# Attention's 64-row matmuls gathered in runs, and layer products handed out chunk by chunk

## Chip, core and metric

The kernel runs on one core of a Trainium2 chip. The metric is the device time of one execution in microseconds (us), the median of several runs. A second number is used below: the profiler's record of one execution, whose span begins with the first and ends with the last recorded instruction.

The engines are TensorE (PE in the profile), its weight loads (PEld), VectorE (DVE), ScalarE (ACT), GpSimd (POOL, idle here) and SyncE (SP), whose queue issues all DMAs. Each engine works through its own instructions in the order in which they stand in the program.

## What is computed

Sigmoid attention, then two feed-forward blocks, all in float32:

```
scores = q @ k.T / sqrt(64) - log(448)         # 4 batches x 12 heads, 448 tokens, head size 64
x = sigmoid(scores) @ v                        # heads laid side by side: 1792 x 768
h = maximum(maximum(x @ w1, x @ w2), x @ w3)   # 768 x 768 each
y = h @ w_out                                  # 768 x 768
t = y @ w_in                                   # 768 x 2048
out = (t * sigmoid(1.702 * t)) @ w_out2        # 2048 x 768
```

## The kernel before

**Precision.** A float32 operand is split into a rounded part (hi) and the rest (lo), and a product is three matmuls: hi by hi, hi by lo, lo by hi. The copies that make hi run on ACT or DVE, whichever the planner gives them to (`copy`); the subtractions that make lo run on DVE alone (`rest`). The six head pairs in `PLAIN` use the sigmoids unsplit.

**Attention.** Two heads make a pair `p`; there are 24 pairs, six to a batch. A pair has four steps `c` over its keys. In steps 0 to 2, `score` issues six matmuls with 64 contraction rows (L412): the two heads lie in rows 0 to 63 and 64 to 127 of the array, and the matmuls of the two heads run side by side, two in the time of one. Step 3 has the last 64 keys of both heads in one 128-row matmul, three times (L414). The scores of a step land in one of two PSUM buffers `sc`, ACT makes the sigmoid `a` from it (L419), and copies and rests make `ah` and `al`. `weigh` multiplies by v into PSUM `av`: 128-row matmuls in steps 0 to 2 (L446, or L438 for plain pairs), 64-row matmuls in step 3 of a pair that isn't plain (L450). `finish` turns `av` into the hi and lo of `x`, one chunk of the contraction (of six) for the first layers.

**Layers.** For each batch `b`, `unit1` runs 18 products for w1, w2, w3 and their maximum, `unit2` six for w_out. Each takes one weight tile `w1` from a ring of five buffers. In batch 0 the tiles are decoded by ACT and DVE (`new_weights`: one ACT and four DVE instructions, then a copy and a rest) and also written to DRAM (`kept`); in batches 1 to 3 they are loaded from there. `product` (L357) issues the 18 matmuls of a tile (six chunks `k`, three each, L363 to L365) as one operation, so it begins only when all six chunks of x are there. Then `unit3` and `unit4` do the last two layers (L553 to L555) over all batches.

**What sets the order.** Nothing is ordered by hand on the engines. The code records operations with what they read and write. `Order.run` then plays a plan: each TensorE operation has a due time (the sum of the planned times of those recorded before it), other operations inherit one from what needs them, and each engine takes the ready operation that is due first. DVE takes a copy that ACT could do as well only as if it were due 12 us later (`SLACK`). The order so found is the program's order, fixed. The order of recording: `step(p, c)` scores step c of pair p and weighs step c of pair p - 1; 28 steps are recorded ahead of the first layer, and the others are spread over the layer units of batches 0 to 2 (L593).

Of the kernel before, what the change touches and what calls it, by code (L numbers as in the profile page):

```python
# [8 lines left out]
F32R = mybir.dt.float32r  # L9
# [6 lines left out]
P = 128  # L16
B, H, S, D = 4, 12, 448, 64
DM = H * D
DFF = 2048
KC = DM // P  # L20
NF = DFF // P
NPAIR = H // 2
NP = B * NPAIR
# [10 lines left out]
MM = 0.201  # L34
# [58 lines left out]
class Order:  # L93
# [35 lines left out]
    def run(self):  # L129
        for r in self.rings:  # L130
            for old, new in zip(r.tiles, r.tiles[r.n :]):
                first = min(new.ops, key=lambda o: o.n)
# [9 lines left out]
        while stack:  # L142
            o = stack.pop()
            seen += 1
            took = min(o.on.values())
# [7 lines left out]
        free = {"PE": 0.0, "ACT": 0.0, "DVE": 0.0, "SP": 0.0, "-": 0.0}  # L153
        need = {o: len(o.pre) for o in self.ops}
# [3 lines left out]
        def offer(o):  # L158
            for e in o.on:
                heapq.heappush(ready[e], (o.late + (SLACK if e == "DVE" and len(o.on) > 1 else 0.0), o.n, o))  # L160
# [5 lines left out]
        while len(done) < len(self.ops):  # L166
            for e in free:
                while free[e] <= now + 1e-9 and ready[e]:
                    _, _, o = heapq.heappop(ready[e])
                    if o in done:  # L170
                        continue
                    done.add(o)
                    o.fn(e)
                    if e == "SP":
                        bus = max(bus, now) + o.on[e]
                        end, free[e] = bus + 2.0, now + 0.07
                    else:
                        end = free[e] = now + o.on[e]
                    o.began, o.end = now, end
                    serial += 1  # L180
                    heapq.heappush(events, (end + o.lag, serial, o))
                    heapq.heappush(events, (free[e], -serial, None))
            assert events, f"{len(self.ops) - len(done)} operations that never begin"
            now = max(now, events[0][0])
            while events and events[0][0] <= now + 1e-9:
                _, _, o = heapq.heappop(events)
                for x in o.post if o is not None else ():
                    need[x] -= 1
                    if not need[x]:
                        offer(x)  # L190


def moe_chain_kernel(tc, qk, vv, v4, wa, wb, out):
# [3 lines left out]
    O = Order()  # L197
# [4 lines left out]
    def ring(p, name, shape, n, dtype=F32, gate=None):  # L202
        return O.ring(n, lambda: p[0].tile(shape, dtype, name=name, tag=name, bufs=n), gate)
# [62 lines left out]
    ]  # L266
    ts, his, los, a2s, a1s, ah2s, ah1s, al2s, al1s, vfs, vss, v4s, xfs, folds = att_rings
    xs = [ring(xp, f"x{k}", [P, 2, S], 2, F32R) for k in range(KC)]
    w1s = ring(xp, "w1", [P, 2, DM], 5, F32R)
    hs = [ring(mid, f"h{k}", [P, 2, S], 1, F32R) for k in range(KC)]  # L270
    mxs = ring(mid, "mx", [P, S], 2)
    yst = ring(mid, "yst", [P, 2, S], 2, F32R)

    def banks(p, name, n, shape=(P, 512)):
        return O.ring(n, lambda: p[0].tile(list(shape), F32, name=name, tag=name, bufs=n))
# [79 lines left out]
        return hi, lo  # L355

    def product(ps, w, x):  # L357
        def f(_):
            wh, wl = w[0](), w[1]()
            for k in range(KC):  # L360
                c = slice(k * P, (k + 1) * P)
                xh, xl = x[k][0](), x[k][1]()
                pe.matmul(ps(), wh[:, c], xh, start=k == 0, stop=False)  # L363
                pe.matmul(ps(), wh[:, c], xl, start=False, stop=False)  # L364
                pe.matmul(ps(), wl[:, c], xh, start=False, stop=k == KC - 1)  # L365

        return O.pe(f, 3 * KC * MM, [*w, *(y for z in x for y in z)], [ps])


    X = [[] for _ in range(B)]  # L370
# [1 line left out]
    class Pair:  # L372
# [27 lines left out]
        def score(self, c):  # L400
# [4 lines left out]
            def f(_):  # L405
                o, h, l = ps(), self.h(), self.l()
                for n, (kx, qx) in enumerate(((h, h), (h, l), (l, h))):
# [5 lines left out]
                    if not pair:  # L413
                        pe.matmul(o, kx[:, keys], qx[:, :S], **how)  # L414

            a, n = (a2s if pair else a1s).tile().part(), (2 if pair else 1) * S
            used = (0, 1 + c // 2) if self.p == 0 else (0,)
            O.pe(f, 3 * MM, [x[i] for x in (self.hi, self.lo) for i in used], [ps])
            on("ACT", t_act(n) + 0.07, lambda: act.activation(a(), ps(), AF.Sigmoid, bias=bias, scale=scale), [ps], [a])  # L419
            self.a[c] = [a]  # L420
            if not self.plain:
# [5 lines left out]
        def weigh(self, c):  # L427
# [22 lines left out]
                            pe.matmul(av[e](), w, x()[r, :], start=False, stop=n == 1)  # L450

            took = (2 if c < 3 else 1) * 0.75 if self.plain else (4 if c < 3 else 2) * MM
            O.pe(plain if self.plain else parts, took, [*self.v, *a], av)
            if c == 3:
                self.finish()

        def finish(self):
            b, hp = divmod(self.p, NPAIR)
# [22 lines left out]

    pairs = [None] * NP

    def step(p, c):
        if p < NP:
            if c == 0:
                pairs[p] = Pair(p)
            pairs[p].score(c)
        if p > 0:
            pairs[p - 1].weigh(c)  # L490


    HS, mx = [None] * KC, [None]
# [88 lines left out]
            pe.matmul(mm_warm(), warm()[:, 0, :P], warm()[:, 1], start=n == 0, stop=n == WARM - 1)  # L582

    O.pe(warming, 3.7, [warm], [mm_warm])
    steps = [(p, c) for p in range(NP + 1) for c in range(4)]
    at = 4 * (NPAIR + 1)
    for s in steps[:at]:
        step(*s)
    order = [(1, m, e) for m in range(KC) for e in range(3)] + [(2, m, 0) for m in range(KC)]
    for b in range(B):  # L590
        first = at
        for n, (layer, m, e) in enumerate(order):
            while b < B - 1 and at < min(len(steps), first + -(-24 * (n + 1) // 22), 28 + 24 * (b + 1)):  # L593
                step(*steps[at])
                at += 1
            unit1(b, m, e) if layer == 1 else unit2(b, m)
    first_ops = {o for r in (*att_rings, scs, avs) for t in r.tiles for o in t.ops}
# [85 lines left out]
```

## Time and profile before

| | us |
|---|---|
| median of 3 runs (1016.23 to 1017.87) | 1017.61 |
| the profiled execution, whole | 1015.61 |
| its recorded span | 1013.8 |
| PE busy in the span | 998.4 |
| DVE busy | 619.5 |
| ACT busy | 360.5 |

The profiled execution was 2.0 us shorter than the median of the three timed runs. The span falls into stretches: attention alone until 65 us, attention with batch 0's layer products and weight decoding until about 198 us, attention with batches 1 and 2 until 442 us, the rest of batches 2 and 3 until 538 us, then the last two layers. A PE that counts as busy is not always at its peak: matmuls overlap, so the distance between the starts of neighbours, not the duration of one, tells the pace.

### The profile page before, as it was taken

The page shows a single profiled execution, that of the slowest core. Times are in us where ns is not written, and L with a number is a line of the kernel's source. Part 1 is how long each engine was busy: PE and PEld are TensorE (multiplying, and loading weights), DVE is VectorE, ACT ScalarE, POOL GpSimd, SP SyncE. Part 2 cuts the span into 40 slices and gives each one's busy share as a digit, 9 for nine tenths or more (in the row PEclk, how much of TensorE's full clock was granted, in tenths as well). Part 3 has the DMA queues.
Part 4 walks back from the last instruction along what each step waited for, and adds up shares of the span by engine and source line. Part 5 has one row for each costly group of instructions (what it writes and reads, how often), then busy time and mean ns, then how long its engine had stood idle before and what let it go on. Part 6 is the DMA issues. An engine that isn't in the chain of part 4 may idle for free.

```text
span 1013.8 us, 12189 instructions
## 1 busy us (share of the span) xinstructions
PE 998.4 (98%) x4918; PEld 864.8 (85%) x4918; DVE 619.5 (61%) x936; ACT 360.5 (36%) x523; POOL 1.1 (0%) x6
## 2 busy tenths in 40 slices
PE   8899999999999999999999999999999999999998
PEld 5457877888888888899998999999999999999997
DVE  6988889865654455455511356776747676664444
ACT  7775767443543444332212342222212122121110
POOL 0000000000000000000000000000000000000000
PEclk9999999999999999999999999999999999999999
DMA  7788677985548554499867211110201111000023
GB/s 253 229 288 285 232 283 288 388 336 170 203 161 289 188 165 140 158 314 414 308 222 274 108 63 63 61 65 1 94 32 63 63 63 63 1 1 1 1 93 125
DMA packets 39656, 165.95 MB, mean 164 GB/s; under 512 B 4400, under 2 KB 10288, under 8 KB 39600
## 3 DMA queue, kind: packets, MB, share of 16 engines
q1 hardware_dynamic: 39600, 165.17, 45.8%
q8 instruction: 39, 0.64, 0.3%
q14 instruction: 17, 0.14, 0.0%
HBM read 129.76 MB, written 35.39 MB: 163 GB/s over the span
## 4 chain that ended last, share of the span: by engine, by line
PE 97%; ACT 1%; DMA 1%; DVE 0%; issue 0%; SPq 0%; DVEq 0%; ACTq 0%
PE mm L363 19%; PE mm L365 19%; PE mm L364 19%; PE po L554 8%; PE po L555 8%; PE po L553 8%; PE av L446 5%; PE sc L412 5%; PE av L438 3%; PE sc L414 1%; PE av L450 1%; ACT a L419 1%; DMA v<-in_v 1%; DMA t<-in_qk 0%; ACT fold L470 0%
## 5 line engine op out<-in xcount | busy, mean ns | idle before, releaser
L363 PE MATMUL mm<-x,w 128*128 128x448 f32 x432 | 161.0, 373 | 0.0
L364 PE MATMUL mm<-x,w 128*128 128x448 f32 x432 | 157.8, 365 | 0.0
L365 PE MATMUL mm<-x,w 128*128 128x448 f32 x432 | 157.6, 365 | 0.0
L553 PE MATMUL po<-g,w 128*128 128x448 f32 x384 | 140.4, 366 | 1.3 <-ACT g L217 1.3
L365 PE MATMUL mm<-z,w 128*128 128x448 f32 x384 | 141.4, 368 | 0.0
L363 PE MATMUL mm<-z,w 128*128 128x448 f32 x384 | 141.3, 368 | 0.0
L364 PE MATMUL mm<-z,w 128*128 128x448 f32 x384 | 141.2, 368 | 0.0
L554 PE MATMUL po<-g,w 128*128 128x448 f32 x384 | 140.4, 366 | 0.2 <-DVE g L220 0.2
L555 PE MATMUL po<-g,w 128*128 128x448 f32 x384 | 140.1, 365 | 0.0
L220 DVE TENSOR_TENSOR acc<-po,acc 128x448 f32<-128x448 f32 (+1 forms) x169 | 104.5, 621 | 53.5 <-PE po L555 52.8
L537 ACT ACTIVATE sg<-mm 128x448 f32<-128x448 f32 x64 | 34.8, 544 | 258.6 <-PE mm L365 258.6
L419 ACT ACTIVATE a<-sc,bias 128x896 f32<-128x896 f32 (+1 forms) x96 | 87.3, 915 | 93.3 <-PE sc L412 68.0
L220 DVE TENSOR_TENSOR al<-a,ah 128x896 fp32r<-128x896 f32 (+1 forms) x72 | 69.7, 974 | 49.2 <-ACT ah L217 48.8
L220 DVE TENSOR_TENSOR gf<-mm,sg 128x448 f32<-128x448 f32 x64 | 39.9, 624 | 97.0 <-ACT sg L537 96.5
L363 PEld LDWEIGHTS mm<-x,w 128*128 128x128 f32 x432 | 81.1, 188 | 10.7 <-issue 3.3
L364 PEld LDWEIGHTS mm<-x,w 128*128 128x128 f32 x432 | 81.2, 188 | 7.3 <-issue 1.1
L365 PEld LDWEIGHTS mm<-x,w 128*128 128x128 f32 x432 | 81.1, 188 | 6.4
L553 PEld LDWEIGHTS po<-g,w 128*128 128x128 f32 x384 | 72.1, 188 | 7.5 <-ACT g L217 1.6
L365 PEld LDWEIGHTS mm<-z,w 128*128 128x128 f32 x384 | 72.2, 188 | 6.8
L364 PEld LDWEIGHTS mm<-z,w 128*128 128x128 f32 x384 | 72.2, 188 | 6.7
L363 PEld LDWEIGHTS mm<-z,w 128*128 128x128 f32 x384 | 72.2, 188 | 6.6
L554 PEld LDWEIGHTS po<-g,w 128*128 128x128 f32 x384 | 72.1, 188 | 6.2 <-DVE g L220 0.5
(76 smaller groups left out, 1363.6 us busy)
## 6 DMA issues: line engine op xcount, KB each, us to landing
w<-kept SPq DMA_DIRECT2D x72, 768.0 KB, 4.8
raw<-in_wb SPq DMA_DIRECT2D x32, 768.0 KB, 5.2
raw<-in_wa SPq DMA_DIRECT2D x24, 768.0 KB, 6.0
kept<-w SPq DMA_DIRECT2D x24, 768.0 KB, 5.3
t<-in_qk SPq DMA_DIRECT2D x23, 480.0 KB, 3.7
yk<-yst SPq DMA_DIRECT2D x24, 448.0 KB, 5.0
z<-yk SPq DMA_DIRECT2D x24, 448.0 KB, 8.5
out_t<-acc SPq DMA_DIRECT2D x23, 224.0 KB, 1.9
```

The source lines that it names most:

```text
L220: return on("DVE", t_two(n), lambda: dve.tensor_tensor(to(), a(), b(), op=op), [a, b], [to])
L363: pe.matmul(ps(), wh[:, c], xh, start=k == 0, stop=False)
L364: pe.matmul(ps(), wh[:, c], xl, start=False, stop=False)
L365: pe.matmul(ps(), wl[:, c], xh, start=False, stop=k == KC - 1)
L412: pe.matmul(o[:, e, :], kx[r, keys], qx[r, :S], **how)
L419: on("ACT", t_act(n) + 0.07, lambda: act.activation(a(), ps(), AF.Sigmoid, bias=bias, scale=scale), [ps], [a])
L438: pe.matmul(o, w, x[:, e, :] if c < 3 else x, start=c + e == 0, stop=c == 3)
L446: pe.matmul(av[e](), w, x()[:, e, :], start=c + n == 0, stop=False)
L537: on("ACT", t_act(S), lambda sg=sg, ps=ps: act.activation(sg(), ps(), AF.Sigmoid, scale=1.702), [ps], [sg])
L553: pe.matmul(ps(), wh[:, c], gh, start=j == 0, stop=False)
L554: pe.matmul(ps(), wh[:, c], gl, start=False, stop=False)
L555: pe.matmul(ps(), wl[:, c], gh, start=False, stop=j == 1)
```

## The change

`beat(n)` takes the place of `step`. Three beats serve two pairs. Each beat begins with a `group`: the 64-row matmuls of two score steps, and with them, where a pair that isn't plain ends, its 64-row weighing of step 3, recorded as one TensorE operation that needs all its inputs and both `sc` buffers. Behind it a beat records the 128-row work: the scores of step 3 (`last_keys`) and the weighing of steps 0 to 2 (`weigh`). Eleven beats stand ahead of the first layer, the other 27 are spread over batches 0 to 2, more densely in batch 1.

`product` records six operations of three matmuls, one for each chunk, so a product may begin when the first chunk of x is there, and others may stand between its chunks. In the planner, a TensorE operation that follows another on TensorE alone no longer waits the planned 0.25 us. The ring of `w1` shrinks from five to four buffers, the ring `yst` grows from two to three.

```diff
-                    heapq.heappush(events, (end + o.lag, serial, o))
-                    heapq.heappush(events, (free[e], -serial, None))
+                    heapq.heappush(events, (end + o.lag, serial, o, False))
+                    heapq.heappush(events, (free[e], -serial, o if e == "PE" else None, True))
...
                 for x in o.post if o is not None else ():
-                    need[x] -= 1
-                    if not need[x]:
-                        offer(x)
+                    if same == ("PE" in o.on and "PE" in x.on):
+                        need[x] -= 1
+                        if not need[x]:
+                            offer(x)
...
-    w1s = ring(xp, "w1", [P, 2, DM], 5, F32R)
+    w1s = ring(xp, "w1", [P, 2, DM], 4, F32R)
...
-    yst = ring(mid, "yst", [P, 2, S], 2, F32R)
+    yst = ring(mid, "yst", [P, 2, S], 3, F32R)
...
     def product(ps, w, x):
-        def f(_):
-            wh, wl = w[0](), w[1]()
-            for k in range(KC):
-                c = slice(k * P, (k + 1) * P)
-                xh, xl = x[k][0](), x[k][1]()
+        for k, (hi, lo) in enumerate(x):
+            c = slice(k * P, (k + 1) * P)
+
+            def f(_, k=k, c=c, hi=hi, lo=lo):
+                wh, wl, xh = w[0](), w[1](), hi()
                 pe.matmul(ps(), wh[:, c], xh, start=k == 0, stop=False)
-                pe.matmul(ps(), wh[:, c], xl, start=False, stop=False)
+                pe.matmul(ps(), wh[:, c], lo(), start=False, stop=False)
                 pe.matmul(ps(), wl[:, c], xh, start=False, stop=k == KC - 1)
 
-        return O.pe(f, 3 * KC * MM, [*w, *(y for z in x for y in z)], [ps])
+            O.pe(f, 3 * MM, [*w, hi, lo], [ps])
...
+    def group(scores, ends=()):
+
+        made = [(p, c, heads(p).score(c)) for p, c in scores if p < NP]
+        whole = [p for p in ends if heads(p).plain]
+        all_ = [m for _, _, m in made] + [heads(p).weigh(3) for p in ends if p not in whole]
+
+        def f(e):
+            for m in all_:
+                m[0](e)
+
+        O.pe(f, sum(m[1] for m in all_) + SWITCH, [x for m in all_ for x in m[2]], [x for m in all_ for x in m[3]])
+        for p, c, m in made:
+            heads(p).scored(c, m[3][0])
+        for p in whole:
+            O.pe(*heads(p).weigh(3))
+        for p in ends:
+            heads(p).finish()
...
+    def beat(n):
+
+        p, part = n // 3 * 2, n % 3
+        if part == 0:
+            group([(p, 0), (p, 1)], [p - 2] if p > 1 else [])
+            weigh(p - 1, 0, 1, 2)
+        elif part == 1:
+            group([(p, 2), (p + 1, 0)], [p - 1] if p > 0 else [])
+            last_keys(p)
+            weigh(p, 0, 1)
+        else:
+            group([(p + 1, 1), (p + 1, 2)])
+            last_keys(p + 1)
+            weigh(p, 2)
...
-    steps = [(p, c) for p in range(NP + 1) for c in range(4)]
-    at = 4 * (NPAIR + 1)
-    for s in steps[:at]:
-        step(*s)
+    beats = NP // 2 * 3 + 2
+    at = 9 + 2
+    for n in range(at):
+        beat(n)
...
-            while b < B - 1 and at < min(len(steps), first + -(-24 * (n + 1) // 22), 28 + 24 * (b + 1)):
-                step(*steps[at])
+            while b < B - 1 and at < min(beats, first + -(-9 * (n + 1) // (17 if b else 22))):
+                beat(at)
                 at += 1
```

What this makes of TensorE's order in batch 1, where layer products (`mm`) and attention alternate. Before (L412 is a 64-row score step of six matmuls, L446 a 128-row weighing):

```order
L412 MATMUL sc_2413<-qh_2189 128x448 x2
L412 MATMUL sc_2413<-ql_2214,qh_2189 128x448 x2
L412 MATMUL sc_2413<-qh_2189,ql_2214 128x448 x2
L446 MATMUL av_2423<-ah2_2273,vs_2212 128x448
L446 MATMUL av_2425<-ah2_2273,vs_2212 128x448
L446 MATMUL av_2423<-al2_2276,vs_2212 128x448
L446 MATMUL av_2425<-al2_2276,vs_2212 128x448
L412 MATMUL sc_2432<-qh_2189 128x448 x2
L412 MATMUL sc_2432<-ql_2214,qh_2189 128x448 x2
L412 MATMUL sc_2432<-qh_2189,ql_2214 128x448 x2
```

After, in the same stage (L413 are the score steps, L454 the 64-row weighing of step 3, L364 the next layer matmul):

```order
L413 MATMUL sc_2566<-qh_2427 128x448 x2
L413 MATMUL sc_2566<-ql_2444,qh_2427 128x448 x2
L413 MATMUL sc_2566<-qh_2427,ql_2444 128x448 x2
L413 MATMUL sc_2573<-qh_2427 128x448 x2
L413 MATMUL sc_2573<-ql_2444,qh_2427 128x448 x2
L413 MATMUL sc_2573<-qh_2427,ql_2444 128x448 x2
L454 MATMUL av_2421<-ah1_2437,vs_2274 128x448
L454 MATMUL av_2423<-ah1_2437,vs_2274 128x448
L454 MATMUL av_2421<-al1_2453,vs_2274 128x448
L454 MATMUL av_2423<-al1_2453,vs_2274 128x448
L364 MATMUL mm_2540<-x4_1545,w1_2389 128x448
```

Two score steps and the weighing of a third pair now stand in one row. In the whole program TensorE's order has 78 unbroken rows of 64-row matmuls before and 38 now; the number of matmuls is the same.

TensorE's order among the first pairs, where attention stood alone. Before (L450 is a 64-row weighing, and no layer matmul stands ahead of the 146th row of the order):

```order
L414 MATMUL sc_289<-qh_201 128x448
L414 MATMUL sc_289<-ql_215,qh_201 128x448
L414 MATMUL sc_289<-qh_201,ql_215 128x448
L450 MATMUL av_252<-ah1_250,vs_147 128x448
L450 MATMUL av_254<-ah1_250,vs_147 128x448
L450 MATMUL av_252<-al1_270,vs_147 128x448
L450 MATMUL av_254<-al1_270,vs_147 128x448
L412 MATMUL sc_306<-qh_258 128x448 x2
```

After (L364 to L366 are a layer product's first chunk, x0, with the first weight tile):

```order
L454 MATMUL av_237<-ah1_263,vs_138 128x448
L454 MATMUL av_239<-ah1_263,vs_138 128x448
L454 MATMUL av_237<-al1_283,vs_138 128x448
L454 MATMUL av_239<-al1_283,vs_138 128x448
L364 MATMUL mm_311<-x0_222,w1_182 128x448
L365 MATMUL mm_311<-x0_222,w1_182 128x448
L366 MATMUL mm_311<-x0_222,w1_182 128x448
L415 MATMUL sc_321<-qh_188 128x448
```

The first chunk of the first product stands among the first pairs' steps, at row 58 of the order.

DVE's order ahead of the last (24th) weight tile that batch 0 decodes. Before (L336 is the last decoding instruction, the last row the tile's rest):

```order
L220 TENSOR_TENSOR al2_1752<-a2_1621,ah2_1689 128x448
L220 TENSOR_TENSOR yst_1748<-mm_1710,yst_1748 128x448
L336 SCALAR_TENSOR_TENSOR y_1706<-raw_1652,y_1706 128x768
L474 TENSOR_TENSOR xf_1789<-av_1613,fold_1780 64x448
L474 TENSOR_TENSOR xf_1789<-av_1615,fold_1783 64x448
L220 TENSOR_TENSOR w1_1793<-y_1706,w1_1793 128x768
```

After:

```order
L221 TENSOR_TENSOR yst_1838<-mm_1794,yst_1838 128x448
L337 SCALAR_TENSOR_TENSOR y_1829<-raw_1748,y_1829 128x768
L221 TENSOR_TENSOR al2_1881<-a2_1708,ah2_1791 128x896
L221 TENSOR_TENSOR vs_1853<-vf_1622,vs_1853 128x7x64
L221 TENSOR_TENSOR al2_1911<-a2_1798,ah2_1860 128x896
L221 TENSOR_TENSOR w1_1906<-y_1829,w1_1906 128x768
```

The tile's rest is DVE's row 231 of the order before and its row 250 now: more of attention's work stands ahead of it.

## Rows read from the trace of the kernel before

**Rows 1.** The profile page's head and part 1: engine, busy us (share), instructions.
```profile
span 1013.8 us, 12189 instructions
PE 998.4 (98%) x4918; PEld 864.8 (85%) x4918; DVE 619.5 (61%) x936; ACT 360.5 (36%) x523; POOL 1.1 (0%) x6
```

**Rows 2.** Stretches: length, busy by engine, granted clock, DMA share, GB/s.
```profile
0.00:65.00 65.00, 58.05 (x265) 33.33 (x266) 52.60 (x75) 48.64 (x64) 1.08 (x6) 1.00 0.74 252
65.00:198.00 133.00, 130.68 (x641) 106.60 (x640) 120.00 (x169) 85.58 (x116) 0.00 (x0) 1.00 0.80 290
```

**Rows 3.** PE's waits over the span: us in total, times, longest.
```profile
PE sc L412 <- ACT a L419: 5.6, 6, 1.4
PE av L438 <- DMA v<-in_v: 1.8, 1, 1.8
...
PE po L553 <- ACT g L217: 1.3, 1, 1.3
PE sc L414 <- ACT a L419: 0.5, 1, 0.5
```

**Rows 4.** Timeline of PE, one 64-row run: start, us, line, tiles, shapes, count.
```profile
252.51 0.37 PE L414 MATMUL sc<-qh,ql 128*128 128x448 f32 x1
252.81 0.47 PE L450 MATMUL av<-ah,vs 64*128 64x448 f32 x2
253.12 0.36 PE L450 MATMUL av<-al,vs 64*128 64x448 f32 x2
253.41 0.47 PE L363 MATMUL mm<-x,w 128*128 128x448 f32 x1
253.72 0.36 PE L364 MATMUL mm<-x,w 128*128 128x448 f32 x1
```

**Rows 5.** Timeline of PE inside a run of two score steps.
```profile
35.79 0.37 PE L412 MATMUL sc<-qh,ql 64*128 64x448 f32 x2
35.99 0.37 PE L412 MATMUL sc<-qh 64*128 64x448 f32 x2
36.20 0.37 PE L412 MATMUL sc<-ql,qh 64*128 64x448 f32 x2
```

**Rows 6.** Timeline of PE: begin of the first and of the last 64-row run.
```profile
5.18 0.47 PE L412 MATMUL sc<-qh 64*128 64x448 f32 x2
...
441.95 0.47 PE L450 MATMUL av<-ah,vs 64*128 64x448 f32 x2
```

**Rows 7.** The page's costliest groups: the sigmoids on ACT; busy, mean ns | idle before.
```profile
L419 ACT ACTIVATE a<-sc,bias 128x896 f32<-128x896 f32 (+1 forms) x96 | 87.3, 915 | 93.3 <-PE sc L412 68.0
```

**Rows 8.** Groups of instructions by line: attention's rests and copies on DVE.
```profile
L220 DVE TENSOR_TENSOR al<-a,ah 128x896 fp32r<-128x896 f32 (+1 forms) x72 | 69.7, 974 | 49.2 <-ACT ah L217 48.8
...
L220 DVE TENSOR_TENSOR vs<-vf,vs 128x448 fp32r<-128x448 f32 x18 | 11.1, 619 | 0.0
...
L217 DVE CAST qh<-t 128x960 fp32r<-128x960 f32 (+1 forms) x17 | 10.5, 615 | 18.7 <-PE sc L414 13.2 <-DMA t<-in_qk 5.5
...
L217 DVE CAST ah<-a 128x896 fp32r<-128x896 f32 (+1 forms) x10 | 5.1, 508 | 0.6 <-ACT a L419 0.5
```

**Rows 9.** DVE's waits from 0 to 198 us, the longest three.
```profile
DVE y L331 <- ACT y L323: 7.4, 8, 1.8
DVE qh L217 <- DMA t<-in_qk: 5.5, 2, 3.7
DVE mx L220 <- PE mm L365: 3.6, 6, 0.9
```

**Rows 10.** Timeline of DVE: the rest of the 24th weight tile.
```profile
187.87 0.96 DVE L220 TENSOR_TENSOR w<-y,w 128x768 fp32r<-128x768 f32 x1 [0.18 <-ACT w L217]
```

**Rows 11.** Timeline of PE: the first matmul with the 24th weight tile.
```profile
192.91 0.36 PE L363 MATMUL mm<-h,w 128*128 128x448 f32 x1
```

**Rows 12.** Timeline of PE: a plain pair's first weighing, behind its load of v.
```profile
71.11 1.77 PE L438 MATMUL av<-a,v 128*128 128x448 f32 x4 [1.84 <-DMA v<-in_v]
```

**Rows 13.** The page's DMA issues: KB each, median us from issue to landing.
```profile
w<-kept SPq DMA_DIRECT2D x72, 768.0 KB, 4.8
```

## What the change should do to the time

> **What bounds the kernel now.** I read the page's busy times first: PE is busy for 998.4 of 1013.8 us, DVE for 619.5 and ACT for 360.5 [rows 1]. So time can only be won where PE works at less than its pace or waits. The list of waits is next: the waits of PE that the profile names for the sigmoids, for a load of v and at the begin of the last layers add up to 5.6 + 0.5 + 1.8 + 1.3 = 9.2 us [rows 3]. That is 1% of the span; the rest must be sought inside the busy time.
>
> The timeline of PE shows it. Among full matmuls the starts are 0.20 us apart, and so are those of 64-row pairs inside a run: 35.79, 35.99, 36.20 [rows 5]. At the two edges of a 64-row run the distances are longer [rows 4]: from the last full matmul (252.51) to the first 64-row pair 0.30, from that to the next pair 0.31, from the last pair (253.12) to the full matmul 0.29, from that to its neighbour 0.31. Each is some 0.10 us more than 0.20, four times: **one run of 64-row matmuls costs 0.41 us on top of its work**, and this run had no wait in it. PE counts as busy meanwhile, so no list of waits shows it. Such runs go from 5.18 to 441.95 us, 78 of them [rows 6]: 78 x 0.41 = 32 us of the busy time are edges.
>
> The third view is DVE by stretches, since it is the engine that the change may load: 52.6 of the first 65 us and 120.0 of the next 133 [rows 2], 90% in the stretch in which it decodes batch 0's weights. Behind that it has room: 619.5 - 52.6 - 120.0 = 447 us in the other 816.
>
> **The change part by part.**
>
> *Grouping.* TensorE's order has 38 runs now, 40 fewer. The steps inside a longer run keep the 0.20 us pace [rows 5], whether they use the same tiles or not, and the number of matmuls stays. All of it is on the path, since PE is: **40 x 0.41 = 16.4 us less**. From below: if a run of three different steps had an edge of its own inside, of half the price, 36 groups would pay some 0.2 us each and 7 us would be left out of 16.4. Rows 5 speak against it, the two steps there write different score buffers and the pace doesn't change; I take 16.4.
>
> *Score buffers.* A group needs both `sc` buffers, so it waits for the sigmoids of the two steps before it, and everything behind it on PE waits too. Two steps take PE 1.2 us (six pairs of 0.20), the two sigmoids take ACT 2 x 0.915 [rows 7]. What covers the difference is the 128-row work between two groups. From the order, at 0.20 us a matmul and some 1.5 us a plain step: 1.5 to 4.4 us ahead of the second to the ninth group, 3.7 us or more (mostly 8 to 10) after that. So only the first groups can wait for ACT, as the single steps did before: the waits for sigmoids came to 6.1 us in 7 waits [rows 3]. The earlier first chunks of the layers now lie among these steps and fill some of that. Bounds: all 6.1 us gone, or as much again. I take no difference, because the work between the first groups is no shorter than that which stood between the single steps there (1.4 to 3 us, worked out alike).
>
> The Trainium skill has a rule against this part. Its page TensorEngine Tiling (Array Packing), section PSUM Bottleneck, says that tiling speeds up TensorE but not the emptying of PSUM, and that the copy out of PSUM can become the bound. The trace shows the same order of sizes here, 1.83 us for ACT against 1.2 for PE; what the rule would make of the time is the first rival below.
>
> *Chunks.* A product was one operation and is six; they carry the same 18 matmuls at the same pace, and no other engine sees the seams. Price nothing; what they bring is the filling just named. They also open two products early, whose weight tiles then stay occupied until the last chunk of x comes.
>
> *Weights in batch 0.* Before, the 24th tile was ready at 187.87 + 0.96 = 188.83 us [rows 10] and first used at 192.91 [rows 11]: 4.1 us to spare. I priced both orders up to these two points by rows. PE has 535 full matmuls, 129 pairs and 36 edges ahead of it before, 550, 146 and 22 now; the plain matmuls are equal. That is 32 x 0.20 - 14 x 0.41 = 0.8 us more: what the edges save there, more attention uses up. DVE has 19 more instructions ahead of it: 11 copies and 8 rests. At 0.51 to 0.62 us a copy and 0.62 to 0.97 a rest [rows 8] that is about 6.2 and 6.4 us. With all of it the tile would be 12.6 - 0.8 - 4.1 = 7.7 us late, and PE, which has it next, would stand. But a copy is given to DVE only where nothing more urgent is ready, so the copies should fall into its waits (7.4 us for ACT's part of the decoding, 5.5 for the first loads, 3.6 for layer products [rows 9]). With the rests alone it is 6.4 - 0.8 - 4.1 = 1.5 us late. Bounds 0 (the rests too go into waits) and 8 us; I take **3 us more**, near the lower end for that reason.
>
> *Four weight buffers instead of five.* From batch 1 on a tile is loaded in 4.8 us [rows 13]. Three others are used meanwhile, 18 matmuls of 0.20 each, 11 us. Covered twice over; if that cover were gone each late tile would cost the difference, some us in all. Nothing.
>
> *v4 has one buffer still.* A plain pair's v is loaded only when the plain pair before has been weighed; that cost 1.8 us once [rows 12]. By the order the work between the two is 4.7 us instead of 4.3. Nothing to 0.4 us won. The third `yst` buffer frees a wait of ACT's that PE doesn't share: nothing. The begin of the last layers has a wait of 1.3 us [rows 3] for the activations; other chunks stand there now that wait for loads instead. I leave it as it is.
>
> **The sum.** 1015.6 - 16.4 + 3 = 1002.2 us for an execution like the profiled one. The runs' median is 2.0 us above that one, so **1004 us** for the median. 0.2% (2 us) is about what a measurement of this kernel can tell from no change.
>
> **The rivals.**
>
> *Slower: the score buffers bind (6%).* If the groups had nothing to cover their sigmoids, each would wait 1.83 - 1.2 = 0.6 us: 36 x 0.6 = 22 us, more than the 16.4 saved, and the median would be 1017.6 - 16.4 + 22 = 1023. It turns the sign once the mean wait of a group is above 16.4 / 36 = 0.46 us. For it: groups ask for both buffers at once, and ACT also makes copies between the sigmoids. It is what the rule on PSUM of the Trainium skill, TensorEngine Tiling (Array Packing), comes to here. Against it: gaps of 8 to 10 us between most groups, and ACT busy for 86 of 133 us [rows 2].
>
> *DVE takes most of it back (8%).* Batch 0's decoding sets the pace: each of the 24 tiles comes late in turn, and 8 to 14 us are lost instead of 3: 1009 to 1016. For it: 90% busy, and 4.1 us to spare where 12.6 us more stand ahead. Against it: by then DVE has waited for 7.4 + 5.5 + 3.6 us and more [rows 9], and nothing forces those waits to stay.
>
> *No change (5%).* The edges are not saved, because the extra 0.10 us is paid by each change of tile inside a group as well, or because waits make up for it by chance: 1016 to 1019.
>
> *Better (5%).* The first chunks fill most of the early waits and DVE is never late: 1004 - 3 - 6 = 995, or under.
>
> **How the numbers follow.** The forecast's own case, 996 to 1009, has 76%. It spans 3 us of DVE less or 5 more than taken and the early waits filled in part. The range of 996 to 1012 adds the nearer half of the DVE case: about 80%. Faster by over 0.2%: 76 + 8 + 5 = 89%. Within 0.2%: 5%. Slower: 6%.
>
> **What would show it.** In the profile of the changed kernel, PE's busy time should be near 982 us, the starts at the edges of a run should still be 0.30 apart and those inside 0.20, over about 38 runs. PE's waits for sigmoids should lie in the first 50 us and not exceed some 6 us. The step on DVE is right if PE's waits for weight tiles or for `al` between 65 and 200 us come to 0 to 8 us, and wrong if there are none or many more. The forecast is wrong if the 64-row pairs inside a run are 0.30 us apart, if groups in batch 1 wait for ACT, or if loads of weights are waited for after 350 us.

## The result, and the profile after

The changed kernel takes **1002.85 us** (median of four runs, 1001.56 to 1004.32) against 1017.37 us for the kernel before in the same comparison (1016.23 to 1017.87): a ratio of 0.9859, 95% interval 0.9842 to 0.9876. The forecast of 1004 us was 1.2 us too high. One of the four executions of `e6_late` below, at 3879.44 us, stands alone and is not counted. The profiled execution of after took 1004.32 us, the longest of its four, with a span of 1002.5 us; span against span the profiles differ by 11.3 us. So the two differences, of medians (14.5) and of profiles (11.3), are not the same, and both have to be explained.

The page's head and its first part for the kernel after (engine, busy us, share, instructions), which answer [rows 1]:

```profile
span 1002.5 us, 12196 instructions
PE 987.9 (99%) x4918; PEld 872.3 (87%) x4918; DVE 621.9 (62%) x945; ACT 347.1 (35%) x514; POOL 1.1 (0%) x6
```

PE has as many matmuls as before and is busy for 10.5 us less: the gain lies inside the busy time. The prediction had expected 982.

The stretches of after that answer [rows 2] (length, busy by engine, clock, DMA share, GB/s):

```profile
0.00:65.00 65.00, 56.82 (x264) 36.75 (x266) 55.06 (x81) 40.84 (x52) 1.08 (x6) 1.00 0.75 261
65.00:198.00 133.00, 131.37 (x676) 109.99 (x673) 123.09 (x174) 91.36 (x127) 0.00 (x0) 1.00 0.74 269
```

In the first 65 us PE is busy for 1.2 us less than before and DVE for 2.5 us more. In the next stretch PE stands for only 1.6 of 133 us.

PE's waits in after (us in total, times, longest), which answer [rows 3]:

```profile
PE av L442 <- DVE xf L476: 2.7, 2, 1.6
PE av L626 <- POOL yst L291: 1.7, 1, 1.7
PE sc L415 <- ACT a L423: 1.6, 1, 1.6
PE av L450 <- DVE x L221: 1.5, 2, 1.0
PE av L442 <- DMA v<-in_v: 1.3, 1, 1.3
PE mm L364 <- DMA z<-yk: 1.1, 1, 1.1
PE av L442 <- ACT a L423: 0.9, 1, 0.9
```

The score steps' waits for sigmoids have shrunk from 6.1 to 1.6 us, or 2.5 with a weighing's wait for one. The first and the fourth line, 4.2 us for DVE's `xf` and `x`, have grown: these sums empty the two `av` banks, and the next weighing waits for them. Before, there was one such line:

```profile
PE av L438 <- DVE xf L474: 0.3, 1, 0.3
```

The sum of the list is 10.8 us, against 11.4. A second profile of after (`e9_after_again`) has 7.5 us: the 4.2 us are there again, the waits for sigmoids are not.

A 64-row run of after in PE's timeline (start, us, line, tiles, shapes, count), beside [rows 4, 5]:

```profile
216.51 0.36 PE L366 MATMUL mm<-x,w 128*128 128x448 f32 x1
216.81 0.47 PE L413 MATMUL sc<-qh 64*128 64x448 f32 x2
217.11 0.36 PE L413 MATMUL sc<-ql,qh 64*128 64x448 f32 x2
217.31 0.36 PE L413 MATMUL sc<-qh,ql 64*128 64x448 f32 x2
217.51 0.37 PE L413 MATMUL sc<-qh 64*128 64x448 f32 x2
217.71 0.36 PE L413 MATMUL sc<-ql,qh 64*128 64x448 f32 x2
217.92 0.37 PE L413 MATMUL sc<-qh,ql 64*128 64x448 f32 x2
218.21 0.47 PE L364 MATMUL mm<-x,w 128*128 128x448 f32 x1
218.53 0.37 PE L365 MATMUL mm<-x,w 128*128 128x448 f32 x1
```

The two distances in and the two out are 0.30, 0.30, 0.29 and 0.32; inside it is 0.20, also where the second step begins (217.31 to 217.51). So a run still costs 1.21 - 0.80 = 0.41 us, and a step more in it costs nothing beyond its 0.20 us a pair. The trace of after has 38 such runs.

**A second pace of full matmuls.** If the edges gave 16.4 us, the busy time should have fallen by more than 10.5. The rest is found where nothing was changed. Stretch 470 to 520 us is nothing but full matmuls at a granted clock of 1.00 in both kernels. Before, in its first profile and in a second one (columns as above):

```profile
470.00:520.00 50.00, 50.00 (x248) 46.33 (x248) 23.87 (x36) 9.85 (x15) 0.00 (x0) 1.00 0.88 322
```
```profile
470.00:520.00 50.00, 50.00 (x249) 46.32 (x248) 25.41 (x38) 9.74 (x15) 0.00 (x0) 1.00 0.89 330
```

After, in its first profile and in a second one:

```profile
470.00:520.00 50.00, 50.00 (x244) 45.42 (x243) 8.74 (x14) 5.46 (x10) 0.00 (x0) 1.00 0.68 228
```
```profile
470.00:520.00 50.00, 50.00 (x244) 45.41 (x243) 8.75 (x14) 5.75 (x11) 0.00 (x0) 1.00 0.66 221
```

Four or five matmuls fewer fit into the same 50 us. Taken over all neighbouring starts of the first layers' products that lie less than 0.23 us apart, `mm` of `x` follows itself after 202.7 ns before and 205.5 ns after (the expectations below put it at 205.7), `mm` of `h` after 202.7 and 205.3. These are means of two values: a stretch runs either at about 203 or at about 207 ns from one interruption (a 64-row run, a plain matmul, a wait) to the next, and in after 767 matmuls in a row from 368 us on have 207. On 1296 matmuls of `x` and 432 of `h` this costs 1296 x 2.8 + 432 x 2.6 ns = 4.8 us. The account of the two profiles is then -16.4 (edges) + 4.8 (pace) - 0.6 (waits) = -12.2 us, against a measured -11.3.

### The profile page after: what moved, and what is told of

Same layout as the page of the kernel before. It is cut to its first block, busy times and chain, and to the rows that moved or that the text cites. A ratio compares the mean times of both kernels' runs of the same rounds, so it can differ in the third digit from the quotient of the medians.

```text
span 1002.5 us, 12196 instructions
## 1 busy us (share of the span) xinstructions
PE 987.9 (99%) x4918; PEld 872.3 (87%) x4918; DVE 621.9 (62%) x945; ACT 347.1 (35%) x514; POOL 1.1 (0%) x6
## 4 chain that ended last, share of the span: by engine, by line
PE 91%; DMA 4%; DVE 3%; issue 1%; ACT 1%; SPq 0%; DVEq 0%
PE mm L364 19%; PE mm L366 19%; PE mm L365 19%; PE po L598 8%; PE po L599 8%; PE po L597 8%; PE sc L413 4%; PE av L450 4%; PE av L442 3%; DMA raw<-in_wa 2%; PE sc L415 1%; PE av L454 1%; DMA v<-in_v 1%; DVE y L337 1%; DVE al L221 0%
## 5 line engine op out<-in xcount | busy, mean ns | idle before, releaser
L364 PE MATMUL mm<-x,w 128*128 128x448 f32 x432 | 162.1, 375 | 0.0
L366 PE MATMUL mm<-x,w 128*128 128x448 f32 x432 | 158.6, 367 | 0.0
L364 PE MATMUL mm<-z,w 128*128 128x448 f32 x384 | 141.5, 368 | 1.1 <-DMA z<-yk 1.1
L366 PE MATMUL mm<-z,w 128*128 128x448 f32 x384 | 141.1, 368 | 0.0
L423 ACT ACTIVATE a<-sc,bias 128x896 f32<-128x896 f32 (+1 forms) x96 | 85.0, 913 | 55.6 <-PE sc L413 43.6
L364 PEld LDWEIGHTS mm<-x,w 128*128 128x128 f32 x432 | 81.1, 188 | 14.8 <-issue 7.3
L366 PEld LDWEIGHTS mm<-x,w 128*128 128x128 f32 x432 | 81.1, 188 | 7.7
L221 DVE TENSOR_TENSOR mx<-mm,mx 128x448 f32<-128x448 f32 x48 | 29.9, 624 | 88.3 <-PE mm L366 88.1
L364 PEld LDWEIGHTS mm<-z,w 128*128 128x128 f32 x384 | 72.2, 188 | 8.2 <-issue 1.4
L366 PEld LDWEIGHTS mm<-z,w 128*128 128x128 f32 x384 | 72.2, 188 | 6.8
```

The lines of the kernel that those rows point to most:

```text
L221: return on("DVE", t_two(n), lambda: dve.tensor_tensor(to(), a(), b(), op=op), [a, b], [to])
```

## The experiments

Four groups, `e1` to `e4`, `e5` to `e8`, `e9` and `e10`, `e11` and `e12`, each ran on one chip and share their runs of the kernel before.

**Cutting the runs open again, and the same work without the cut.** In 36 groups a matmul with 64 columns, whose result the next one overwrites, is put ahead of the second score step: in `e1_cut` over 128 rows, so that the run is cut in two (74 runs), in `e2_nocut` as a 64-row pair (38 runs).

```diff
-            for m in all_:
+            for i, m in enumerate(all_):
+                if i == 1 and len(made) > 1:
+                    (q, _, mm), h = made[1], heads(made[1][0])
+                    o = mm[3][0]()
+                    for e_ in range(1):                    # e2_nocut: range(2)
+                        z = slice(0, P)                    # e2_nocut: slice(e_ * D, (e_ + 1) * D)
+                        pe.matmul(o[:, e_, :64], h.h()[z, S : S + P], h.h()[z, :64], start=True, stop=True)
                 m[0](e)
```

> The changed kernel with one more matmul ahead of the second score step of each of its 36 full groups: a 128-row matmul of 64 columns into that step's score buffer, which the step's own first matmul overwrites. That cuts each run of 64-row matmuls in two: 74 runs instead of 38. The added matmul itself costs a weight load, some 0.2 us. Theory (each run costs 0.41 us at its edges): 36 x (0.2 + 0.41) = 22 us more than the changed kernel, 1025 us, and 15 us more than the run without the cut (e2_nocut). Rival (the gain came from the spacing, the chunks or the early filling, not from fewer edges): the same time as e2_nocut within 4 us.

> The same additional matmul as in e1_cut, but as a pair of 64-row matmuls, one for each head, so that the run of 64-row matmuls isn't cut: 38 runs. Both theories: 36 x 0.2 = 7 us more than the changed kernel, about 1010 us. It is the control that e1_cut is read against.

Measured: `e1_cut` 1011.54 us, ratio to before 0.9945 (0.9927 to 0.9963); `e2_nocut` 1002.46 us, 0.9857 (0.9835 to 0.9880). Both are far below the 1025 and 1010 us expected. Against `e2_nocut` the cut costs 9.1 us, where 15 were expected. PE's timeline of `e1_cut` at a cut (L506 is the added matmul):

```profile
221.98 0.38 PE L413 MATMUL sc<-qh,ql 64*128 64x448 f32 x2
222.29 0.30 PE L506 MATMUL sc<-qh 128*128 128x64 f32 x1
222.52 0.47 PE L413 MATMUL sc<-qh 64*128 64x448 f32 x2
222.83 0.36 PE L413 MATMUL sc<-ql,qh 64*128 64x448 f32 x2
```

The same place in `e2_nocut`:

```profile
218.46 0.36 PE L413 MATMUL sc<-qh,ql 64*128 64x448 f32 x2
218.66 0.19 PE L506 MATMUL sc<-qh 64*128 64x64 f32 x2
218.69 0.45 PE L413 MATMUL sc<-qh 64*128 64x448 f32 x2
218.97 0.36 PE L413 MATMUL sc<-ql,qh 64*128 64x448 f32 x2
```

From the last pair of one step to the second of the next it is 0.40 us in after (217.31 to 217.71), 0.85 with the cut and 0.51 without; the medians over the 36 places are 0.40, 0.83 and 0.51. The added matmul is worth 0.11 us as a pair, less than the 0.2 that I had put in the expectation, and the cut 0.32 us more than that, three quarters of the 0.41 us of a whole run. On 36 groups that is 11.5 us between the two; the profiles differ by 8.9. Two things make up the difference. PE's waits sum to 5.9 us in `e1_cut` and to 10.5 in `e2_nocut`, 4.6 us less; among them are those for `xf` and `x`, first with the cut, then without:

```profile
PE av L442 <- DVE xf L476: 1.9, 2, 1.1
PE av L450 <- DVE x L221: 0.5, 1, 0.5
```
```profile
PE av L442 <- DVE xf L476: 2.6, 2, 1.4
PE av L450 <- DVE x L221: 1.1, 2, 0.7
```

And the products' mean pace, `x` and `h` together, is 203.9 ns against 202.9, 1728 x 1.0 ns = 1.7 us more: 11.5 - 4.6 + 1.7 = 8.6. So an edge that is put back costs time on the spot, and the rival, that the two kernels are the same, is out; but the kernel with more edges waits less, for `xf` and `x` 2.4 us instead of 3.7. In `e2_nocut` the added 4.0 us are made up against after by the pace of 202.9 ns instead of 205.5 (-4.5 us).

**Each half alone.** `e3_steps` is the kernel before with the chunks, the new rule of the planner and the new ring sizes, but single score steps (79 runs). `e4_whole` is the kernel after with whole products (37 runs).

```diff
# e3_steps, against before (the planner's rule, as in the change, is not repeated)
...
+        for k, (hi, lo) in enumerate(x):
...
+            O.pe(f, 3 * MM, [*w, hi, lo], [ps])
...
-    w1s = ring(xp, "w1", [P, 2, DM], 5, F32R)
+    w1s = ring(xp, "w1", [P, 2, DM], 4, F32R)
...
-    yst = ring(mid, "yst", [P, 2, S], 2, F32R)
+    yst = ring(mid, "yst", [P, 2, S], 3, F32R)
# e4_whole, against after
...
-            O.pe(f, 3 * MM, [*w, hi, lo], [ps])
+        return O.pe(f, 3 * KC * MM, [*w, *(y for z in x for y in z)], [ps])
```

> The kernel before with everything of the change but the groups and beats: products in six chunks, the planner's rule for TensorE followers, w1 with four and yst with three buffers. The order has 79 runs of 64-row matmuls. Theory (edges): no edge is saved; at most the early waits are filled, so 1012 to 1019 us. Rival (chunks and rings bring the gain): 1003 to 1008 us.

> The changed kernel with products as one operation again; groups, beats and rings as changed, 37 runs of 64-row matmuls. Theory (edges): 41 x 0.41 = 17 us under the kernel before, plus 0 to 4 us of early waits that no first chunk fills: 1001 to 1005 us. Rival (the chunks bring a good part): 1010 us or more. In the changed kernel's profile the first layers' matmuls start 206 ns apart instead of 203; if the chunks are the reason, this kernel has 203 again and is 3 to 5 us faster than it would be.

Measured: `e3_steps` 1012.99 us, 0.9965 (0.9952 to 0.9978); `e4_whole` 1004.81 us, 0.9879 (0.9858 to 0.9901). The change without the chunks brings 12.3 us, the chunks with the planner's rule and the rings alone 4.1; of these some 1.6 are the clock, since nine of the 17 executions of before ran at a mean clock of 0.998 or less and only two of the twelve of `e3_steps` (at 0.999 or more the medians are 1015.4 and 1012.9). What shows the chunks as filling is that without them PE waits 6.8 us for `xf` and `x` instead of 4.2. The expectation's question on the pace has two answers: `e4_whole` is back at a mean of 203.1 ns, but `e2_nocut` has its chunks and 202.9. So chunks alone don't set the pace.

**Is it DVE?** `e5_light` has after's order, but leaves out DVE's shift in the decoding of batch 0's weights (the last bits of those weights are then wrong): 24 instructions of 1.04 us, 25 us less work for DVE.

```diff
-            lambda: dve.tensor_scalar(half(2), half(1), 13, None, op0=ALU.logical_shift_right),
+            lambda: None if light else dve.tensor_scalar(half(2), half(1), 13, None, op0=ALU.logical_shift_right),
```

> The changed kernel, same order on every engine, without the shift (one DVE instruction of 0.8 us) that makes the lowest bits of each weight in batch 0's decoding; this part of the computation is left out, so the last bits of w1, w2, w3 and w_out are off. DVE is 24 x 0.8 = 20 us lighter in the first 198 us. Theory (DVE takes back part of what the edges save): PE's waits for DVE in the first 65 us of the changed kernel's profile (2.7 us for xf, 1.5 for x) go for the greater part, 2 to 4 us less, 999 to 1001. Rival (those waits are set by ACT or PE itself and DVE is no bound): 1002 to 1003 us, the same waits.

Measured: 1000.37 us (999.25 to 1000.71), 0.9841 (0.9824 to 0.9858). Every execution is shorter than the eight of after (1001.27 to 1004.77), the medians by 2.5 us, though the intervals of the ratios overlap. The size is what the theory said, the place is not shown. The waits for `xf` and `x` fell only from 4.2 to 3.4 us. The list fell from 10.8 to 8.0 us in all, but after's own second profile has 7.5, with no wait for a sigmoid and 0.4 us for v, so the rest of the fall says nothing. That DVE takes back part of the gain is shown by the waits for `xf` and `x`, 4.2 us in both profiles of after against 0.3 before; how much a lighter DVE would return stays open, between 0.8 and 2.5 us.

**Can the planner do better?** `e6_late` no longer adds 0.25 us between PE's steps when due times are made. `e8_model` tells it that the shift takes 0.95 us instead of 0.555 (the trace shows 1.04).

```diff
# e6_late
-            late = min((x.late - took - o.lag for x in o.post), default=1e9)
+            late = min(
+                (x.late - took - (0.0 if "PE" in o.on and "PE" in x.on else o.lag) for x in o.post), default=1e9
+            )
# e8_model: the duration given for the shift
-            t_one(DM),
+            0.95,
```

> The changed kernel with one more correction in the planner: a chunk that follows another on TensorE is due without the planned 0.25 us between them. The last chunk of a product then stands ahead of the first chunk of the next, not behind it. Theory (chunk order is free of cost): within 1.5 us of the changed kernel, and both paces of full matmuls (203 and 207 ns) still occur in the profile. Rival (two products interleaved set the slower pace): 203 ns throughout and 3 to 5 us less, 998 to 1000.

> The changed kernel with the planner told that the shift in the weight decoding takes 0.95 us on DVE, as the profile shows, instead of the 0.555 us that it assumes. Theory (DVE's late xf in the first 65 us come from that short figure): its waits on PE's path shrink from 4.2 us to 1 to 3, 1000 to 1002 us. Rival (DVE's work there is simply too much): the waits stay in sum, 1002 to 1004 us.

Measured: `e6_late` 1002.48 us (median of three, 1002.36 to 1003.51), 0.9866 (0.9847 to 0.9886); `e8_model` 1004.37 us, 0.9881 (0.9865 to 0.9897). Neither is better than after, and in both the waits for `xf` and `x` stay, at 4.4 to 4.7 us. `e6_late` also frees the pace from one suspicion: chunks of two products no longer alternate in it, and both paces are still there (205.7 ns on average).

**The rings.** `e7_rings` is after with the old ring sizes.

```diff
-    w1s = ring(xp, "w1", [P, 2, DM], 4, F32R)
+    w1s = ring(xp, "w1", [P, 2, DM], 5, F32R)
-    yst = ring(mid, "yst", [P, 2, S], 3, F32R)
+    yst = ring(mid, "yst", [P, 2, S], 2, F32R)
```

> The changed kernel with the rings of before: five w1 buffers, two yst buffers. Theory (rings cost and bring nothing): within 1.5 us of the changed kernel, 1001 to 1004 us. Rival (the fifth buffer lets DVE decode further ahead and so covers it): no wait for xf or x in the first 65 us and 2 to 4 us less.

Measured: 1007.17 us (1005.63 to 1012.51), 0.9916 (0.9893 to 0.9939), 4.3 us more than after. This was a miss. Its list of PE's waits has a line that neither before nor after has:

```profile
PE mm L364 <- DVE yst L221: 2.6, 2, 1.5
```

PE stands at 438 and 443 us, since the product's bank isn't empty. ACT's timeline there names the one that comes last (in brackets the wait):

```profile
437.11 0.53 ACT L218 CAST yst<-mm 128x448 fp32r<-128x448 f32 x1 [5.92 <-DMA yk<-yst]
442.11 0.53 ACT L218 CAST yst<-mm 128x448 fp32r<-128x448 f32 x1 [4.47 <-DMA yk<-yst]
```

With two `yst` buffers ACT's copy out of the bank waits until a transfer has read the buffer, DVE's rest waits for the copy, and PE for both. The waits sum to 14.3 us, against 10.8 and 7.5 in after's two profiles; the profiled execution also has a stretch at a low clock like those shown below. The two ring sizes were not tried one by one; the line names `yst`.

**The same kernels again.** A second profile of each tells whether the pace belongs to the program or to chance.

> The changed kernel once more, unaltered, for a second profile. Its full matmuls of the first layers ran 205.7 ns apart on average in its first profile (767 in a row at 207 ns from 368 us on), against 202.7 in the profile of the kernel before. If the pace belongs to the order of the program, the second profile shows 205.7 within 0.3 ns and the same long stretch at 207. If it falls out by chance at each interruption of an execution, the mean is another value between 202.7 and 206.7 and the long stretch can be at 203, which would make the execution up to 4 us shorter than 1004.3 us.

> The kernel before once more, unaltered, for a second profile. Its first profile was the fastest of its executions, 1015.6 us, with all full matmuls of the first layers 202.7 ns apart. If the pace belongs to the program: 202.7 within 0.3 ns again, and an execution near 1015.6. If it is chance: some stretches at 207 ns, a mean above 203, and an execution of 1017 to 1019 us, the extra time being 1580 matmuls times the difference of the means.

Measured: after 1002.91 us, 0.9866 (0.9844 to 0.9888); before 1015.71 us, 0.9997 (0.9984 to 1.0009). The mean paces of `x` are 205.4 and 202.6 ns, and the stretch of 767 at 207 ns is there again. Of 32 longer stretches of after 25 have the same pace in both profiles; the seven others all lie between 176 and 240 us, behind the wait of 1.6 us at 173 us that only the first profile has. So the pace mostly goes with the order of the program; where it changes, a wait stands ahead, though that the wait is the reason is not shown. The waits of the second profile of after for `xf`, `x` and v are:

```profile
PE av L442 <- DVE xf L476: 2.7, 2, 1.6
PE av L450 <- DVE x L221: 1.5, 2, 1.0
PE av L442 <- DMA v<-in_v: 0.4, 1, 0.4
```

The second part of the expectation for `e10_before_again` failed: its profiled execution was the longer one after all, 1017.85 us, at the same pace. Its rows show why. PE's timeline behind the load of v that [rows 12] show (in brackets the wait):

```profile
71.72 2.64 PE L438 MATMUL av<-a,v 128*128 128x448 f32 x4 [2.14 <-DMA v<-in_v]
73.48 1.25 PE L363 MATMUL mm<-x,w 128*128 128x448 f32 x1
74.53 0.57 PE L364 MATMUL mm<-x,w 128*128 128x448 f32 x1
74.90 0.57 PE L365 MATMUL mm<-x,w 128*128 128x448 f32 x1
75.28 0.57 PE L363 MATMUL mm<-x,w 128*128 128x448 f32 x1
```

And the stretch of that execution around it:

```profile
73.00:76.00 3.00, 3.00 (x8) 2.00 (x7) 2.98 (x5) 2.39 (x3) 0.00 (x0) 0.52 0.79 238
```

The wait was 2.14 us long, and behind it the granted clock is 0.52, the lower level of 1.2 GHz: full matmuls start 0.37 us apart. In the first profile of before the same wait was 1.84 us [rows 12], the clock stayed at 1.00, and the four plain matmuls took 1.77 us. The episode sets the execution back by some 2 us. The 17 executions of before beside `e1_cut` fall into groups by their mean granted clock: eight at 1.000 or 0.999 took 1015.0 to 1016.0 us, four at 0.998 took 1017.1 to 1018.3, five at 0.996 took 1018.8 to 1019.9. The four executions of after in the first comparison are all at 1.000 or 0.999. Its median is 12.5 us below that of those eight (1015.4), so of the 14.5 us between the medians about 2 are the clock of before's executions.

**Freeing the banks first.** `e11_first` gives the steps behind `xf` and `x` an early due time; `e12_late_first` does so on top of `e6_late`. Both compute everything.

```diff
-                copy(xh, self.av[0], S, psum=True)
-                rest(xl, self.av[0], xh, S)
+                copy(xh, self.av[0], S, psum=True).at = O.clock - 4
+                rest(xl, self.av[0], xh, S).at = O.clock - 4
...
                 on("ACT", t_act(S), lambda f=f, av=av: act.copy(f(), av()[D:]), [av], [f])
+                O.ops[-1].at = O.clock - 4
...
-                )
+                ).at = O.clock - 4
```

> The changed kernel with the steps that free attention's weighing banks (xf, x) given a due time at their group, 4 us ahead, so that the planner no longer puts a weight's decoding in front of them; nothing is left out. Theory: PE's waits for xf and x (4.2 us in the first 60 us, two profiles) come from DVE's order there. They should fall to 1 to 3 us, and the median to 1000 to 1002 us. Rival: DVE is short of time there in any order, the waits stay at 4 us or turn up as waits for al or for weight tiles, and the median stays within 1 us of 1002.9.

> The same due times on top of the planner of e6_late (chained steps of PE without 0.25 us between them), whose wait of 3.07 us for xf at 26 us was followed by a stretch at a granted clock of 0.57, in which eight plain matmuls took 4.97 us instead of 3.27. Theory: a wait shorter than the 1.64 us of the changed kernel leaves the clock at 1.00; that wait here below 1.6 us, the clock 1.00 throughout, and a median of 999 to 1001 us, 2 to 4 below e6_late's 1003.0. Rival: the clock falls there whatever the wait, or the wait moves to the next bank, and the median is 1002 to 1004.

Measured: `e11_first` 1003.19 us (998.45 to 1004.48), 0.9864 (0.9845 to 0.9884): the rival holds, the waits for `xf` and `x` are 3.8 us and new ones of 0.9 and 1.2 us came elsewhere. `e12_late_first` 1000.58 us (998.22 to 1003.67), 0.9850 (0.9831 to 0.9870), the lowest median of a kernel that leaves nothing out; its interval still overlaps that of after. The median lies where the theory had it, but not for its reason. Its longest wait for `xf` is not below 1.6 us:

```profile
PE av L444 <- DVE xf L479: 3.8, 2, 2.8
```

and the clock fell behind it, to 0.50 between 28 and 30 us. What it has that `e6_late` lacks is a faster pace, 203.5 against 205.7 ns, worth 1728 x 2.2 ns = 3.8 us, more than its lead of 1.9 us; its waits sum to 8.2 us against 7.6. So the due times have not won the lead by shorter waits. Whether the new order brought the faster pace is not shown.

## Why the prediction came out right, point by point

*Edges, -16.4 us.* Right in number (38 runs) and in price (0.41 us, steps inside 0.20). `e4_whole` shows that the change without the chunks keeps most of the gain, and `e1_cut` beside `e2_nocut` that an edge put back costs 0.32 us on the spot.

*Score buffers, no difference (bounds -6.1 to +6.1).* It came out on the good side of the bounds: the sigmoids' waits went from 6.1 to 2.5 us, in the second profile to none, and the first chunks now stand in the gaps. No group in batch 1 waits for ACT (PE's only wait behind 198 us is 1.1 us for a load), so the rule on PSUM (the Trainium skill, TensorEngine Tiling (Array Packing), PSUM Bottleneck) didn't come to bear. The one wait that lies later than expected is 1.6 us at 173 us, in the first profile alone.

*DVE, +3 us.* The size was right by luck (the waits for `xf` and `x` have grown by 3.9 us), the place was wrong. I had followed the 24th weight tile (32 x 0.20 - 14 x 0.41 is 0.7 us there and not 0.8, which changes nothing). Its rest on DVE in after:

```profile
194.80 0.96 DVE L221 TENSOR_TENSOR w<-y,w 128x768 fp32r<-128x768 f32 x1
```

and PE's first matmul with it:

```profile
195.90 0.47 PE L364 MATMUL mm<-h,w 128*128 128x448 f32 x1
```

It is ready 0.14 us ahead of its use: where [rows 10, 11] had 4.1 us to spare nothing is left, but PE doesn't stand. PE's waits for weight tiles or `al` between 65 and 200 us are none, which by the prediction's own words makes this step wrong. What DVE did cost lies in the first 60 us, where it is busy for 55 of 65: the sums that free the `av` banks come behind the decoding there (4.2 us of PE's waits). The step that failed is that only the weight tiles and `al` were followed, and not the banks that DVE also has to empty.

*Chunks and the rings, nothing.* The chunks are probably worth more than nothing: with whole products the median is 2 us longer, although the faster pace gives 1728 x 2.4 ns = 4.1 us back, and the waits for `xf` and `x` are 2.6 us longer; a part of the time may be the clock, 0.995 to 0.998 in the executions of `e4_whole`. The step on the third `yst` buffer failed: "frees a wait of ACT's that PE doesn't share" was read from the old order, and in the new one PE shares it (`e7_rings`). The four weight buffers are right for after: no load of a weight is waited for. They are not for every order: with the same four, `e3_steps`, `e11_first` and `e12_late_first` wait 2.9, 1.2 and 1.4 us for loads of weights.

*v4, 0 to 0.4 us.* 1.8 us became 1.3 in the first profile of after and 0.4 in the second.

*PE's busy time near 982.* 987.9. The step that failed is that the full matmuls of the layers would keep their pace; 4.8 us went there, and no term of the sum or bound allowed for it.

*The median 2.0 us above the profile.* It was taken over from before, where it goes with the clock: about half of before's executions are at a mean of 0.998 or less and take 2 or 4 us longer, and after's four were not. After's profiled execution, 1004.3 us, is above its median. So the profile's own time was forecast 2.1 us too low (1002.2) and the step to the median 3.5 us too high. The closeness of 1004 to 1002.85 owes something to these two errors of opposite sign. There is such luck inside the first of them too: the pace, which was not in the sum, added 4.8 us, and the waits, for which the sum had +3, changed by -0.6.

## What to carry to other kernels

A cost that sits inside the busy time, as the edges here, is found in the distances of starts and can be counted; it is won in full on the spot, but engines that had time enough at the old pace can take part of it back, so look for every buffer and bank that the next busiest engine must free, not only for the data that it delivers. Price a ring by the order that will use it, not by the one that is profiled. And put two profiles of the same kernel beside each other before a difference of 2 us is given a cause, as `e5_light` shows.

## What was not expected of the hardware

**Two paces.** Full matmuls of 448 columns run at about 203 or about 207 ns at a granted clock of 1.00, the same from one interruption to the next, and mostly the same in two profiles of one program. Neither of two suspects sets it alone. Chunks that alternate are not needed for the slow pace: `e6_late` and the whole products of `e4_whole` have both. Nor does the load on the DMA queues decide: before has 203 at a DMA share of 0.88 and after 207 at 0.68, but `e2_nocut` has 203 at nearly the share of after:

```profile
470.00:520.00 50.00, 50.00 (x249) 46.33 (x248) 9.02 (x15) 6.01 (x11) 0.00 (x0) 1.00 0.67 228
```

The last two layers, whose code the change leaves alone, have both paces before and after, in all four profiles of the two kernels: from some 570 us on every fourth of the long rows of `z` matmuls runs at 203, the three between at 206. In `e7_rings` the 18 matmuls between the two waits for `yst` ran at 203, the stretch before them and the 428 behind at 207. What sets the pace at an interruption stays open; it is worth up to 5 us here, a third of the gain.

**The clock behind a wait.** Behind PE's first long wait for `xf` the eight plain matmuls of `e6_late` and of after took different times. PE's timeline of `e6_late`:

```profile
29.19 4.97 PE L444 MATMUL av<-a,v 128*128 128x448 f32 x8 [3.07 <-DVE xf L478]
```

and its stretch from 30 to 34 us:

```profile
30.00:34.00 4.00, 4.00 (x7) 1.54 (x5) 3.94 (x7) 1.38 (x2) 0.00 (x0) 0.57 0.69 245
```

PE's timeline of after, and the same stretch:

```profile
28.56 3.27 PE L442 MATMUL av<-a,v 128*128 128x448 f32 x8 [1.64 <-DVE xf L476]
```
```profile
30.00:34.00 4.00, 4.00 (x19) 2.10 (x18) 3.94 (x7) 2.31 (x4) 0.00 (x0) 1.00 0.79 281
```

So a wait of 3.07 us cost another 1.7 us at 1.2 GHz, and one of 1.64 us nothing. The length of the wait alone doesn't decide: in `e7_rings` the clock fell behind a wait of 1.68 us at the same place, and before it stayed at 1.00 behind one of 1.84 us [rows 12].
